# Seam between routing and experts: zeros in TensorE's waits, expert 0's weight blocks loaded in routing, the read of the output's row numbers written behind expert 2

## The chip, the cores and the metric

The program runs on 1 core of one Trainium2 chip. The metric is the time of one execution on the device in microseconds (us); of several runs the median is given. Engines are written as in the profile: PE is TensorE's matmul, PEld its weight load, DVE is VectorE, ACT ScalarE, POOL GpSimd, SP SyncE, whose queue issues most of the DMA. L12 is line 12 of the kernel.

## What is computed

Three stages follow one another; between them nothing leaves the device.

```python
def _attn_ref(q, k, v, s):                 # q, k, v (4, 8, 576, 64), s (4, 8, 576)
    scores = scale * np.matmul(q, k.transpose(0, 1, 3, 2))
    cum = np.cumsum(np.maximum(s, 0.0), axis=-1)
    bias = -(cum[:, :, :, None] - cum[:, :, None, :])
    scores = np.where(causal, -1000000000.0, scores + np.minimum(bias, 0.0))
    attn = softmax(scores)
    return np.matmul(attn, v)

def _moe_ref(x, w_gate, w1, w2):           # x (2304, 512), 8 experts, w1 (8, 512, 1024), w2 (8, 1024, 512)
    cap = N // E                           # 288 tokens for each expert
    for idx in np.argsort(-(x @ w_gate).flatten()):
        tok, e = idx // E, idx % E
        if assigned[tok] < 0 and counts[e] < cap:
            assigned[tok] = e; counts[e] += 1
    for e in range(E):
        out[assigned == e] = np.maximum(x[assigned == e] @ w1[e], 0.0) @ w2[e]

def _moe2_ref(x, w_in, w_out):             # w_in (512, 2048), w_out (2048, 512)
    h = x @ w_in
    return (h * (1.0 / (1.0 + np.exp(-1.702 * h)))) @ w_out
```

`w_in` and `w_out` arrive as 64-bit floats, which the kernel takes apart as pairs of 32-bit integers.

## The kernel before, in words

**Attention and routing.** The first 230 us or so compute attention and write its 2304 rows (each batch padded to 580 rows, five tiles of 116) to `x_rows` in DRAM. Routing then finds, for each expert, the cut above which its 288 tokens lie: rounds of comparisons on VectorE (L468 to L479) and small matmuls on TensorE (L624, L631). `fill_slots` (from L688) turns the assignment into a list: matmuls for positions (L696 to L698), tables `inv` and `lane` on VectorE, ScalarE and POOL (L710 to L717), 20 matmuls that turn them into row numbers (`pid`, L721), and `gather(0)` (L665), three indirect DMAs of POOL that fetch the 288 rows of expert 0. Then it issues matmuls of zeros (`pulse`, L682 to L686: a 128 x 128 block of zeros times 128 x 512 zeros, results not used). While routing computes, SP loads blocks 0 and 1 of expert 0's weights (`load_w`, L498) and two pieces of `w_in` (`first64`).

**Seam.** Behind routing `output_rows` (L760) works out where each row of the result goes, and SP writes these 2304 four-byte numbers to `o_rows` in DRAM (L767). They are read back in another layout into `oids` (L971). The numbers are wanted only at the very end of the kernel, when rows are scattered to the output.

**Experts.** For each expert e the gathered rows are transposed in three groups (`gather_t`, L866) and split into a high and a low half (`xT`: ScalarE L868, VectorE L869). The hidden layer is made in eight column blocks m: `up(e, m)` (L876) issues 12 first products (three products of halves for each of four blocks of the inner dimension; for e = m = 0 smaller ones), ScalarE takes the relu's high half (L891), VectorE the low half `hT` (L892). `down(e, m)` (L895) issues 12 second products (L899) into four PSUM banks. Weights come in four blocks g = m // 2 of 512 KB for w1 and 512 KB for w2; `weights(e, g)` splits them into halves (ScalarE L774, VectorE L775), and their raw tiles `wraw` have four buffers. Beside this run conversions of `w_in` and `w_out` ("jobs"): a DMA of a raw piece (L798, tile `raw64`, two buffers), five integer steps on VectorE (L801 to L810) and one on ScalarE (L804), and a split into halves `win`. Products of `up` and the transposes share four PSUM banks named h, used in turn. So a group of transposes waits until VectorE has read the bank that it is given.

**What sets the order.** Routing up to `fill_slots` is in an order written by hand (`manual_schedule`). From the seam on, the order on each engine, SP's and POOL's queues included, is set by a scheduler that goes by priorities, the text's order and its own cost estimates; the text's place of a DMA is only a hint. Each engine then runs its list in order.

Of the kernel before, what the change touches and what calls it, by code (L numbers as in the profile page):

```python
# [8 lines left out]
F32 = mybir.dt.float32  # L9
# [29 lines left out]
JS = 96  # L39
# [8 lines left out]
def tile_kernel(ctx, tc, qt, kt, v, s, w_gate, w1, w2, w_in, w_out, out):  # L48
# [446 lines left out]
    raws = {}  # L495

    def load_w(e, g):
        r1 = wp.tile([128, 4, 256], F32, name="wraw", bufs=4)  # L498
        if (e, g) == (0, 2):

            G.tensor_copy(r1[:JS, 0, :1], xT["g", 2][:, :1])
        SY.dma_start(r1, w1[e, :, g * 256:(g + 1) * 256].rearrange("(k p) f -> p k f", p=128))
        r2 = wp.tile([128, 2, DM], F32, name="wraw", bufs=4)
        SY.dma_start(r2, w2[e, g * 256:(g + 1) * 256].rearrange("(k p) f -> p k f", p=128))
        raws[e, g] = r1, r2

    load_w(0, 0)
    load_w(0, 1)

    first64 = []  # L510
    for g in range(2):
# [147 lines left out]
    xT = {}  # L659
# [23 lines left out]
    def pulse(n, start=False, W=128):  # L683
        p = rps.tile([128, 512], F32, name="warm", bufs=1) if rps else warm[0]
        for i in range(n):
            PE.matmul(p[:, :4 * W], zeros, zeros[:, None, :W].to_broadcast([128, 4, W]), start=start and i == 0, stop=bool(rps) and i == n - 1)  # L686

    def fill_slots(check=True):  # L688
# [8 lines left out]
        PE.matmul(pos, tri, oh, start=False, stop=False)  # L697
        PE.matmul(pos, ones, incl, start=False, stop=True)  # L698
        if check:
            V.tensor_reduce(cnt, all_, axis=AX.X, op=OP.add)  # L700
        V.tensor_tensor(sl, pos, oh, op=OP.mult)
        if check:
# [158 lines left out]
    def gather_t(e):  # L861
        x = wp.tile([128, 2, 4, CAP], F32R, name="xT")
        for j in range(3):
            p = bank("h")[:, :4 * JS].rearrange("p (d j) -> p d j", d=4)
            for d in range(4):
                PE.transpose(p[:, d], xT["g", 3 * e + j][:, d * 128:(d + 1) * 128], identf[:JS, :JS])  # L866
            o = slice(j * JS, (j + 1) * JS)
            hi = A.activation(x[:, 0, :, o], p, AF.Copy)  # L868
            lo = V.tensor_tensor(x[:, 1, :, o], p, f32(x[:, 0, :, o]), op=OP.subtract)  # L869
        xT[e] = x  # L870
        return hi, lo
# [62 lines left out]
    jobs_ = run_jobs(wp, PM)  # L934
    ws[0, 0] = weights(0, 0)
    warm = [bank("h")]
    pulse(2, True)
    for ins in gather_t(0):
        ctx.enter_context(tc.issue_after(ins.ins))
    for e in range(E):  # L940
        py = [bank(f"y{d}")[:, :CAP] for d in range(4)]
# [25 lines left out]
            A.activation(yt[:, d], py[d], AF.Copy)  # L967
        SY.dma_start(y_dram[:, :, e * CAP:(e + 1) * CAP], yt)
        yt = new_yt()
        if e == 0:  # L970
            SY.dma_start(oids, o_rows.rearrange("(c p) o -> p (c o)", p=128))  # L971
        if e in (0, 1):
            for f in load_y(e, wp):
# [286 lines left out]
```

## Time and profile before

| | |
|---|---|
| runs | 901.83, 906.05, 905.21 us; median 905.21 |
| profiled execution | 903.1 us; span from first to last instruction 901.3 us; mean granted clock of TensorE 0.962 |
| busy, share of the span | PE 94%, DVE 80%, ACT 56%, POOL 31% |
| DMA | 124.37 MB, mean 138 GB/s |
| expert 0's first product to its last group of first products | 272.3 to 309.05 us |

The span is divided into stages with different limits; attention ends near 230 us, routing near 264, the seam near 272, the experts follow one another at some 27 us each, and the second MLP comes last. Busy shares over the whole span say little about the seam; for that one reads timelines (start, duration, engine, line, operation, result and operands, and behind it in brackets how long the engine stood idle before it and what released it) and windows (busy time of each engine in a stretch, the granted TensorE clock as a share of full speed, and the share and rate of DMA).

### The profile page before, as it was taken

To read this page: it belongs to the slowest core of one execution; us is meant where nothing else is said; L and a number is where in the kernel's file an instruction comes from. 1 tells how busy PE (TensorE), PEld (TensorE's weight loads), DVE (VectorE), ACT (ScalarE), POOL (GpSimd) and SP (SyncE) were. 2 spreads that over 40 slices of the span, in tenths; PEclk is the share of its full clock that TensorE was granted. 3 is DMA by queue.
4 is the path that set the end of the run, shared out by engine and by line. 5 is a ranking of instruction groups with operands and counts; after the bars stand their busy time and mean duration, and the time that the engine had idled before them with its cause. 6 is when DMAs were issued, how large, how long until landed. Compare 5 with 4: busy or idle time off the path is not lost.

```text
span 901.3 us, 18540 instructions
## 1 busy us (share of the span) xinstructions
PE 844.4 (94%) x6838; PEld 825.6 (92%) x6838; DVE 723.0 (80%) x1683; ACT 508.7 (56%) x1141; POOL 277.3 (31%) x264
## 2 busy tenths in 40 slices
PE   4899999999559899999999999999999999999997
PEld 3799999999438899999999999999999999999996
DVE  4688888889774679889998589998877987777775
ACT  5899998988433457666575343434435444444432
POOL 2999999973241110031100011111000211111112
PEclk9799999999657799999999999999999999999999
DMA  6886549520517778888875433323255211111101
GB/s 155 195 204 184 147 118 235 126 80 1 166 34 125 231 234 272 254 255 264 259 227 191 138 106 106 111 72 123 83 184 195 84 48 47 48 48 48 48 24 48
DMA packets 88389, 124.37 MB, mean 138 GB/s; under 512 B 10540, under 2 KB 56768, under 8 KB 87780
## 3 DMA queue, kind: packets, MB, share of 16 engines
q1 hardware_dynamic: 85156, 113.55, 43.2%
q0 software_dynamic: 3136, 9.57, 3.5%
q8 instruction: 56, 0.92, 0.4%
q14 instruction: 41, 0.34, 0.1%
HBM read 96.61 MB, written 22.21 MB: 132 GB/s over the span
## 4 chain that ended last, share of the span: by engine, by line
PE 43%; DVE 13%; DMA 5%; issue 5%; ACT 3%; POOL 1%; POOLq 0%; DVEq 0%; SPq 0%; ACTq 0%
PE h L1002 13%; PE y L1034 10%; PE y L899 9%; PE h L889 9%; DVE g L1020 3%; DVE gT L1212 2%; ACT gT L1208 1%; DMA wraw<-in_moe_w_dram 1%; DMA raw<-in_moe_w_in_dram 1%; DMA raw<-in_moe_w_out_dram 1%; DVE g L1014 1%; DMA wi_dram<-wist 1%; DVE part L1065 1%; DVE tmp L1065 1%; PE h L866 1%
## 5 line engine op out<-in xcount | busy, mean ns | idle before, releaser
L1002 PE MATMUL h<-yc,win 128*128 128x256 f32 x1728 | 218.6, 283 | 0.0
L1002 PEld LDWEIGHTS h<-yc,win 128*128 128x128 f32 x1728 | 212.4, 192 | 0.0
L1034 PE MATMUL y<-wout,gT 128*128 128x256 f32 x1491 | 189.6, 282 | 6.8 <-DVE part L1065 4.2
L1034 PEld LDWEIGHTS y<-wout,gT 128*128 128x128 f32 x1491 | 180.8, 189 | 9.4 <-issue 3.5
L1208 ACT ACTIVATE gT<-g 128x896 fp32r<-128x896 f32 x72 | 68.4, 949 | 139.6 <-DVE g L1020 138.7
L889 PE MATMUL h<-xT,w1s 128*128 128x288 f32 (+2 forms) x776 | 119.3, 303 | 4.0 <-DVE w1s L775 3.9
L899 PE MATMUL y<-hT,w2s 128*128 128x288 f32 x768 | 116.3, 300 | 0.9 <-DVE hT L892 0.5
L889 PEld LDWEIGHTS h<-xT,w1s 128*128 128x128 f32 x776 | 111.1, 196 | 4.9 <-DVE w1s L775 4.4
L899 PEld LDWEIGHTS y<-hT,w2s 128*128 128x128 f32 x768 | 107.8, 192 | 1.5 <-DVE hT L892 1.0
L217 DVE TENSOR_TENSOR phl<-pt,phl 116x464 fp32r<-116x464 f32 (+1 forms) x128 | 76.1, 598 | 27.1 <-ACT phl L212 26.9
L1212 DVE TENSOR_TENSOR gT<-g,gT 128x896 fp32r<-128x896 f32 x72 | 78.8, 1095 | 16.4 <-ACT gT L1208 16.3
L1020 DVE TENSOR_TENSOR g<-g 128x128 f32<-128x128 f32 x284 | 75.2, 306 | 4.9
L228 PE MATMUL pt<-phl,vhl 116*128 116x232 f32 (+2 forms) x512 | 76.1, 292 | 1.7 <-POOL vhl L92 1.6
L665 POOL DMA_INDIRECT xg<-x_rows,idx x24 | 29.7, 1237 | 146.7 <-PE h L866 139.5
L212 ACT ACTIVATE phl<-pt 116x464 fp32r<-116x464 f32 (+1 forms) x128 | 69.1, 540 | 9.9 <-PE pt L206 9.7
L228 PEld LDWEIGHTS pt<-phl,vhl 116*128 116x128 f32 x512 | 67.0, 195 | 3.2 <-POOL vhl L92 2.2
L1069 POOL DMA_INDIRECT out_dram<-part,oids x18 | 22.3, 1237 | 150.4 <-DVE part L1065 150.4
L1009 ACT ACTIVATE sg<-h 128x256 f32<-128x256 f32 x84 | 32.0, 383 | 64.0 <-PE h L1002 62.5
L206 PE MATMUL pt<-identf,pr 116*116 116x116 f32 x480 | 65.8, 268 | 0.7 <-DVE phl L217 0.7
L1010 DVE TENSOR_TENSOR g<-h,sg 128x256 f32<-128x256 f32 x84 | 35.5, 423 | 32.8 <-ACT sg L1009 32.3
L165 PE MATMUL sc<-x 128*116 128x348 f32 (+3 forms) x192 | 44.9, 343 | 15.5 <-ACT x L115 11.1
L206 PEld LDWEIGHTS pt<-identf,pr 116*116 116x116 f32 x480 | 51.5, 141 | 4.1 <-PE sc L174 1.0
(192 smaller groups left out, 1427.8 us busy)
## 6 DMA issues: line engine op xcount, KB each, us to landing
wraw<-in_moe_w_dram SPq DMA_DIRECT2D x64, 512.0 KB
yraw<-y_dram SPq DMA_DIRECT2D x18, 512.0 KB
raw<-in_qt_dram SPq DMA_DIRECT2D x30, 290.0 KB
raw<-in_kt_dram SPq DMA_DIRECT2D x30, 290.0 KB
raw<-in_moe_w_in_dram SPq DMA_DIRECT2D x32, 256.0 KB
raw<-in_moe_w_out_dram SPq DMA_DIRECT2D x32, 256.0 KB
y_dram<-yt SPq DMA_DIRECT2D x8, 576.0 KB
vraw<-in_v_dram SPq DMA_DIRECT2D x16, 280.0 KB
```

The source lines that it names most:

```text
L165: PE.matmul(p[:, c0:c0 + w], X[x][:, 0, t * P:(t + 1) * P], X[x][:, 1, k0:k0 + w], start=x == 0 and banks[m] not in banks[:m], stop=x == 1 ...
L206: PE.transpose(p[:, w - P:w], pr[:, place(t, c):place(t, c + 1)], identf[:P, :P])
L212: A.activation(hl[:, 0], p, AF.Copy)
L217: st["lo", i] = V.tensor_tensor(hl[:, 1], st["pt", i, g], f32(hl[:, 0]), op=OP.subtract)
L228: PE.matmul(p[:, t0 * P:(t0 + n) * P], vhl[:, hh, c].rearrange("p a d -> p (a d)"), st["phl", i, g][:, x, col:col + n * P], start=x == 0 a ...
L889: PE.matmul(p[:, o], w[:, a, k, c], x[:, b, k, o], start=n == 0 and (e, m) != (0, 0), stop=n == len(steps) - 1)
L899: PE.matmul(py[d], w[:, a, m % 2, d * 128:(d + 1) * 128], h[:, b], start=m == 0 and n == 0, stop=m == 7 and n == 2)
L1002: PE.matmul(h, w[:, a, k], yc[c][:, b, k], start=n == 0 and (both is None or half == 0), stop=n == 11 and (both is None or half == 1))
L1020: V.tensor_tensor(g[:, o], g[:, a], g[:, b], op=op)
L1034: PE.matmul(acc[b][:, o * 256:o * 256 + 256], t[:, j, x], wout[:, p, i, y], start=p == 0 and n == 0 and b not in banks[:m], stop=end and n ...
L1208: A.activation(t[:, 0, :n], src, AF.Copy)
L1212: V.tensor_tensor(t[:, 1, :n], src, f32(t[:, 0, :n]), op=OP.subtract)
```

## The change

Blocks 2 and 3 of expert 0's weights go into tiles that are free at that time: one of the tag `comb` and one of the tag `xT`. They are so loaded in routing with blocks 0 and 1. A small copy on POOL (L501), which tied the load of block 2 to the gathered rows, is gone. Seven zeros matmuls are put behind the position matmuls of `fill_slots`, one more (three in place of two) ahead of the first transposes, and four, one and two behind the three groups of transposes of expert 0; the zeros and transposes there are held in the text's order on TensorE. The read of `o_rows` is written behind expert 2 in place of expert 0.

```diff
     def load_w(e, g):
-        r1 = wp.tile([128, 4, 256], F32, name="wraw", bufs=4)
-        if (e, g) == (0, 2):
-
-            G.tensor_copy(r1[:JS, 0, :1], xT["g", 2][:, :1])
+
+        spare = {(0, 2): ("comb", 1), (0, 3): ("xT", 2)}.get((e, g))
+        if spare:
+            both = wp.tile([128, 2, 1024], F32, name="wraw_" + spare[0], tag=spare[0], bufs=spare[1])
+            r1, r2 = both[:, 0].rearrange("p (k f) -> p k f", k=4), both[:, 1].rearrange("p (k f) -> p k f", k=2)
+        else:
+            r1 = wp.tile([128, 4, 256], F32, name="wraw", bufs=4)
+            r2 = wp.tile([128, 2, DM], F32, name="wraw", bufs=4)
         SY.dma_start(r1, w1[e, :, g * 256:(g + 1) * 256].rearrange("(k p) f -> p k f", p=128))
-        r2 = wp.tile([128, 2, DM], F32, name="wraw", bufs=4)
         SY.dma_start(r2, w2[e, g * 256:(g + 1) * 256].rearrange("(k p) f -> p k f", p=128))
         raws[e, g] = r1, r2
 
     load_w(0, 0)
     load_w(0, 1)
+    load_w(0, 2)
+    load_w(0, 3)
...
         PE.matmul(pos, ones, incl, start=False, stop=True)
         if check:
+            pulse(7, True)
+        if check:
             V.tensor_reduce(cnt, all_, axis=AX.X, op=OP.add)
...
                 PE.transpose(p[:, d], xT["g", 3 * e + j][:, d * 128:(d + 1) * 128], identf[:JS, :JS])
+            if e == 0:
+                pulse((4, 1, 2)[j])
             o = slice(j * JS, (j + 1) * JS)
...
     warm = [bank("h")]
-    pulse(2, True)
-    for ins in gather_t(0):
+    with tc.manual_schedule(engines={PE.engine}):
+        pulse(3, True)
+        first_split = gather_t(0)
+    for ins in first_split:
         ctx.enter_context(tc.issue_after(ins.ins))
...
-        if e == 0:
+        if e == 2:
             SY.dma_start(oids, o_rows.rearrange("(c p) o -> p (c o)", p=128))
```

SP's queue in the seam, before. (`wraw_4818` and `wraw_4821` are block 2 of expert 0, `wraw_4895` and `wraw_4897` its block 3, `wraw_4983` block 0 of expert 1; `raw64` are pieces of `w_in`.)

```order
L767 DMA o_rows_4707<-oidx_4706 96x24x1
L502 DMA wraw_4818<-in_moe_w1_dram 128x4x256
L504 DMA wraw_4821<-in_moe_w2_dram 128x2x512
L971 DMA oids_4708<-o_rows_4707 128x18x1
L502 DMA wraw_4895<-in_moe_w1_dram 128x4x256
L504 DMA wraw_4897<-in_moe_w2_dram 128x2x512
L502 DMA wraw_4983<-in_moe_w1_dram 128x4x256
L798 DMA raw64_4959<-in_moe2_w_in_dram 128x4x128
L798 DMA raw64_5059<-in_moe2_w_in_dram 128x4x128
```

The same stretch of SP's queue in the changed kernel. (`wraw_5007` and `wraw_5008` are block 0 of expert 1, `wraw_5146` and `wraw_5147` its block 1.)

```order
L774 DMA o_rows_4729<-oidx_4728 96x24x1
L506 DMA wraw_5007<-in_moe_w1_dram 128x4x256
L507 DMA wraw_5008<-in_moe_w2_dram 128x2x512
L982 DMA oids_4730<-o_rows_4729 128x18x1
L506 DMA wraw_5146<-in_moe_w1_dram 128x4x256
L507 DMA wraw_5147<-in_moe_w2_dram 128x2x512
L805 DMA raw64_4983<-in_moe2_w_in_dram 128x4x128
L805 DMA raw64_5083<-in_moe2_w_in_dram 128x4x128
```

Blocks 2 and 3 of expert 0 are gone from it and blocks 0 and 1 of expert 1 stand in their places; one load fewer stands ahead of the third `raw64`. The read of `oids` stands behind the same number of loads as before.

VectorE around the conversion of the third piece of `w_in`, before. (`hT_4918` is the low half for m = 4, `hT_4956` for m = 5; `w1s_4899` is the split of block 3's w1, `w2s_4826` of block 2's w2.)

```order
L801 TENSOR_SCALAR u64_4961<-raw64_4959 128x256
L805 SCALAR_TENSOR_TENSOR u64_4961<-raw64_4959,u64_4961 128x256
L775 TENSOR_TENSOR w1s_4899<-wraw_4895,w1s_4899 128x1024
L807 SCALAR_TENSOR_TENSOR u64_4961<-raw64_4959,u64_4961 128x256
L775 TENSOR_TENSOR win_4729<-w64_4927,win_4729 128x4x64
L775 TENSOR_TENSOR w2s_4826<-wraw_4821,w2s_4826 128x1024
L810 SCALAR_TENSOR_TENSOR w64_4967<-t64_4963,u64_4961 128x256
L892 SCALAR_TENSOR_TENSOR hT_4918<-h_4905,hT_4918 128x288
```

The same in the changed kernel. (`hT_4942` is the low half for m = 4, `hT_4980` for m = 5; `w1s_4923` is block 3's w1, `w2s_4854` block 2's w2, `raw64_4983` the third piece.)

```order
L782 TENSOR_TENSOR w1s_4923<-wraw_xT_3634,w1s_4923 128x1024
L782 TENSOR_TENSOR win_4751<-w64_4907,win_4751 128x4x64
L817 SCALAR_TENSOR_TENSOR w64_4951<-t64_4947,u64_4945 128x256
L782 TENSOR_TENSOR w2s_4854<-wraw_comb_3631,w2s_4854 128x1024
L901 SCALAR_TENSOR_TENSOR hT_4942<-h_4929,hT_4942 128x288
L808 TENSOR_SCALAR u64_4985<-raw64_4983 128x256
L782 TENSOR_TENSOR win_4751<-w64_4951,win_4751 128x4x64
L812 SCALAR_TENSOR_TENSOR u64_4985<-raw64_4983,u64_4985 128x256
L901 SCALAR_TENSOR_TENSOR hT_4980<-h_4967,hT_4980 128x288
```

The first step that reads the third piece has moved from ahead of these two weight splits to behind them and behind the low half for m = 4; it stands directly ahead of a `win` half, a second step on the piece and the low half for m = 5.

## Rows read from the trace of the kernel before

**Rows 1.** Windows: stretch, length, busy us (instructions) per engine, granted clock, DMA share, GB/s.

```profile
272.00:280.00 8.00, 8.00 (x37) 7.77 (x36) 3.51 (x6) 3.40 (x7) 2.78 (x3) 0.50 0.63 31
280.00:281.00 1.00, 1.00 (x8) 1.00 (x8) 1.00 (x4) 0.34 (x1) 0.00 (x0) 0.85 0.90 117
297.00:298.00 1.00, 0.00 (x0) 0.00 (x0) 1.00 (x2) 1.00 (x3) 0.00 (x0) 0.68 0.00 0
307.00:308.00 1.00, 1.00 (x8) 1.00 (x7) 1.00 (x3) 0.00 (x0) 0.00 (x0) 0.70 0.91 237
309.00:520.00 211.00, 210.71 (x1628) 210.24 (x1627) 178.32 (x351) 126.45 (x237) 21.73 (x17) 1.00 0.74 231
```

**Rows 2.** Timeline of PE in experts 0 and 1: start, duration, operation, [idle before].

```profile
298.52 2.77 PE L889 MATMUL h<-xT,w1s 128*128 128x288 f32 x10 [3.38 <-DVE w1s L775]
...
302.73 0.90 PE L866 MATMUL h<-identf,xg 96*128 96x96 f32 x4 [0.16 <-issue]
303.34 5.87 PE L899 MATMUL y<-hT,w2s 128*128 128x288 f32 x28
309.05 1.75 PE L889 MATMUL h<-xT,w1s 128*128 128x288 f32 x12
...
331.79 3.98 PE L899 MATMUL y<-hT,w2s 128*128 128x288 f32 x28
335.61 1.75 PE L889 MATMUL h<-xT,w1s 128*128 128x288 f32 x12
```

**Rows 3.** Timeline of PE in the seam.

```profile
261.30 2.20 PE L721 MATMUL pid<-inv,lane 116*96 116x48 bf16 x20 [3.39 <-POOL inv L714]
263.33 3.52 PE L686 MATMUL warm<-zeros 128*128 128x512 bf16 x8
...
268.82 0.52 PE L866 MATMUL h<-identf,xg 96*128 96x96 f32 x4 [0.78 <-DMA xg<-x_rows,idx]
270.82 1.51 PE L866 MATMUL h<-identf,xg 96*128 96x96 f32 x8 [1.47 <-issue]
```

**Rows 4.** Windows of routing and of the last loads of expert 0.

```profile
233.00:248.00 15.00, 7.26 (x75) 5.39 (x75) 11.73 (x55) 5.58 (x18) 6.41 (x10) 0.50 0.78 250
248.00:264.00 16.00, 7.70 (x71) 5.91 (x72) 13.47 (x49) 6.31 (x15) 6.41 (x8) 0.50 0.02 6
289.00:297.00 8.00, 5.62 (x38) 5.17 (x38) 1.95 (x7) 2.27 (x6) 0.00 (x0) 1.00 0.86 262
```

**Rows 5.** Timeline of POOL in the seam.

```profile
264.84 1.07 POOL L665 DMA_INDIRECT xg<-x_rows,idx  x1 [2.32 <-issue]
...
271.45 0.18 POOL L501 COPY wraw<-xg 96x1 f32<-96x1 f32 x1 [3.08 <-DVE orow L765]
```

**Rows 6.** SP's queue in expert 0: start and duration of the issue.

```profile
283.26 0.37 SPq L971 DMA_DIRECT2D oids<-o_rows  x1
283.73 4.83 SPq L502 DMA_DIRECT2D wraw<-in_moe_w_dram  x1
288.67 0.45 SPq L504 DMA_DIRECT2D wraw<-in_moe_w_dram  x1
```

**Rows 7.** SP's waits, 260 to 312 us: total us, times, longest.

```profile
SPq L971 <- DMA o_rows<-oidx: 9.5, 1, 9.5
```

**Rows 8.** Timeline of DVE in expert 0.

```profile
296.58 0.29 DVE L801 TENSOR_SCALAR u<-raw 128x256 int32<-128x256 int32 x1 [6.01 <-DMA raw<-in_moe_w_in_dram]
296.91 0.42 DVE L805 SCALAR_TENSOR_TENSOR u<-raw,u 128x256 int32<-128x256 int32 x1
...
301.09 0.42 DVE L775 TENSOR_TENSOR win<-w,win 128x256 fp32r<-128x256 f32 x1
301.43 0.42 DVE L805 SCALAR_TENSOR_TENSOR u<-raw,u 128x256 int32<-128x256 int32 x1
...
302.23 0.45 DVE L892 SCALAR_TENSOR_TENSOR hT<-h,hT 128x288 fp32r<-128x288 f32 x1
```

**Rows 9.** Timeline of ACT in expert 0.

```profile
291.69 1.06 ACT L774 ACTIVATE w1s<-wraw 128x1024 fp32r<-128x1024 f32 x1 [2.22 <-DMA wraw<-in_moe_w_dram]
```

## Prediction, made before the changed kernel ran

> **What bounds the kernel now.** I read the windows first, then the timelines of the engine that bounds each stretch. From 309 us on TensorE is never free: 210.71 of the 211 us to 520 are busy, at full granted clock [rows 1]. So whatever arrives earlier at 309 shifts the rest of the program, and the question is only how early expert 0 can be done. Its end is marked by the last first-product group (`up(0,7)`), which starts at 309.05 behind the third group of transposes of expert 1 (at 302.73, called T2 here) and 28 second products [rows 2].
>
> Expert 0 is slow for three reasons, each visible in a row. TensorE waited 3.38 us for the weight half `w1s` of block 3, until 298.52 [rows 2]. The granted clock was 0.50 of full (the lower of the two levels, 1.2 GHz) from 272 to 280, while TensorE was busy all of it, and rose at about 280.3 (0.85 in that microsecond); behind the idle stretch it fell again (0.68 in 297 to 298) and rose at 307.6 (0.70 in 307 to 308) [rows 1]. What would expert 0 take without these? The same 28 second products that took 5.71 us there (303.34 to 309.05) took 3.82 us in expert 1 (331.79 to 335.61), 0.1364 us each [rows 2]. From the first product of expert 0 (272.3, where the last transposes of [rows 3] end) to `up(0,7)` stand 84 first products, 72 second ones and 12 transposes of a third of the columns, together 160 such units: 21.8 us at full clock against 36.8 us taken. The difference of 15.0 us is all that can be won here.
>
> **The change, part by part.**
> *Seven zeros behind the position matmuls.* A zeros matmul costs 3.52/8 = 0.44 us [rows 3], at the lower clock that this stretch has [rows 4], so 3.1 us. TensorE stands idle there for 3.39 us, until `inv` of POOL releases it at 261.30 [rows 3]. Cost 0; if POOL were earlier, at most 3.1 us.
>
> *Four loads in routing instead of in the seam.* They are 4 x 524 kB. The loads that stand there now ran at 250 GB/s until about 248; then DMA moved 6 GB/s until 264 [rows 4]. So the four take 2097 kB / 250 GB/s = 8.4 us, until about 256.5, and the gather of expert 0's rows is issued only at 264.84 [rows 5]. Cost 0; the cover is 8 us wide. The two new homes (the tiles of `comb` and of the second `xT`) are wanted again only later, by expert 1. The removed copy on POOL took 0.18 us and nothing waited for POOL there [rows 5]: 0.
>
> *Eight zeros more in the seam (one before the first transposes, 4, 1 and 2 behind the three groups).* The four fall into a wait of 1.47 us between the first and second group [rows 3]: 0.9 us at full clock, nothing lost; at half clock 1.76 us, 0.3 lost. The three behind cost 0.66 us at full clock, 1.3 at half. The gain they may bring is the first half-clock stretch: 8 us of work done in 4. No row shows the clock in the seam with these zeros in it, so both ends are kept: the clock full from 268 on, or as before.
>
> *The waits on blocks 2 and 3.* Their loads are issued some 30 us or more earlier now, so the 3.38 us wait of TensorE goes. Next late is something else, and the order shows what.
>
> *The row numbers of the output.* The text of the program has them behind expert 2, but in SP's queue their read stands where it stood, behind the two loads that follow the writing. SP will be held there as before: 9.5 us until 283.26 [rows 6, 7]. The next load of w1 was then held for 4.83 us more, and w2's followed at 288.67 for 0.45 us [rows 6]; the four transfers ahead of them are alike in number and size in both kernels, so I take the same. The third piece of `w_in` (`raw64`) now stands behind those two and is issued at 289.2. In front of it are 2 x 524 kB, with its own 262 kB 1311 kB, which at the 262 GB/s of 289 to 297 [rows 4] takes 5.0 us: it lands at about 294.2 (before: 296.5, where VectorE's first reading of it starts at 296.58 [rows 8]).
>
> *Who waits for that piece.* VectorE runs in order. Before, its conversion stood in front of the last weight splits; now it stands in front of the low half of `hT` for m = 5, and T2 needs the PSUM bank that this reads. Behind the landing come the conversion's first step, a `win` half, the second step and `hT`: by the starts of such rows 3 x 0.33 us, and 0.45 us for the last [rows 8], in sum 1.45. So T2 starts at about 295.6, not at 302.73: this **new wait** takes the place of the old one. In before too `hT` for m = 5 ended at 302.68, T2 starting 0.05 us later [rows 2, 8].
>
> *From T2 to `up(0,7)`.* Three cases. (A) The zeros keep the clock up: TensorE has 132 units less, so it is at T2 at 272.3 + 0.66 + 18.0 = 291.0, stands 4.6 us idle, the clock falls as it did behind the idle stretch of 3.38 us, and T2 to `up(0,7)` takes the 6.32 us of before [rows 2]: 301.9, a gain of 7.1. (B) The zeros don't help: TensorE is at T2 at about 295.1, hardly idle, and the 28 products run at full clock: 295.6 + 4.4 = 300.0, a gain of 9.1. (C) As B, and the zeros themselves delay the first product by 1.3 us at half clock: about 301.1, a gain of 8.0. The two half-clock stretches trade against the new wait, so all three lie close: I take 8.0.
>
> *Where the sum stands.* The profiled execution took 903.1 us (span 901.3), 2.1 below the median of 905.21. 903.1 - 8.0 = 895.1, and with the 2.1 us 897.2. From A and B, and 0.7 for the DMA rate, the forecast's own range is 895.5 to 899.5.
>
> The Trainium skill ("Trainium Kernel Development and Optimization", Key Constraints) says that DMAs of all queues run on the same 16 engines and interleave. If the pieces behind it in the queue shared the rate with the third piece of `w_in`, it would end with the fourth, 262 kB later. This case's rows bear that out only in part: w1 of block 3, issued by 288.56, was used at 291.69 [rows 9], 3.1 us on, while 524 kB alone take 2.0 us and all that was issued up to 290.7 needs until 296.5.
>
> **The rivals.**
> 1. *The landing is shared.* The piece lands together with the one behind it, 262 kB or 1.0 us later, at 295.2; T2 and `up(0,7)` follow by 1.0 to 1.2: 898.4. For it: four transfers are in flight at once. Against it: the row on w1 just named.
> 2. *No new wait.* SP was held 4.83 us with w1's buffer long read, so that hold may belong to the queue's state and be shorter now. With the piece issued below 284.5 it lands before TensorE wants T2. With the clock up: 272.3 + 0.66 + 21.8 = 294.8, a gain of 14.2: 891.0. Against it: the same write and the same two loads are in front.
> 3. *Part is lost.* The piece lands at 296.5 as before, T2 starts at 298.0, `up(0,7)` 6.32 us later at 304.3: a gain of 4.7, 900.5. Or the clock falls in the new wait and stays down for some 7 products after `up(0,7)` has begun, 0.14 us each: near 901 as well. For it: in before the clock needed until 307.6, 9 us from the work's start at 298.5.
> 4. *Slower.* One mechanism: SP. Everything that VectorE waits for now hangs behind the reading of the row numbers. Break-even is `up(0,7)` at 309.05, that is T2 at 302.7 and the piece landing at 301.2; from 305.7 on the kernel is over 0.5% slower. If the 9.5 and 4.83 us of holding both last twice as long, because the loads in the seam compete with four-byte writes, the piece lands at 294.2 + 14.3 = 308.5 and the time is 903.1 + 7.3 + 2.1 = 912.5. For it: 9.5 us for a 9 kB write is long already. Against it: the seam now has fewer, not more, bytes that are wanted.
> 5. *The change does less than it says.* For the row numbers that is already so by the order, and counted in the sum. A load that could not start in routing would be seen as a wait at 284; the rows of POOL and DMA give no reason.
>
> **How the numbers follow.** The forecast (A to C) has 0.50, rival 1 0.10, rival 2 0.10, rival 3 0.20, rival 4 0.08, and 0.02 is left for what I don't see. 0.5% is 4.5 us, about what a measurement of this kernel can tell from no change: faster means below 900.7, slower above 909.7. Faster takes the forecast, rivals 1 and 2 and a third of rival 3: 0.76. Same takes the rest of rival 3 and what I don't see, 0.16; slower 0.08. The range runs from rival 2 (891.0, 0.5 below for its clock) to the upper side of rival 3 without the tail: 890.5 to 902.5. It leaves out rival 4, some of rival 3, and little else.
>
> **What would show it right or wrong.** Right: TensorE's 3.38 us wait on `w1s` gone; SP reads the row numbers near 283 and issues the third `raw64` near 289; VectorE waits on that piece until about 294; T2 near 295.6 and `up(0,7)` between 300 and 302, with the second products of the other experts at 0.136 us each. The granted clock of 272 to 280 tells A from B and C. Wrong: T2 before 292 (rival 2), after 297 (rival 3), after 302.7 (rival 4), or a shift at 309 that isn't there at the end, which would mean that a later stage waits for something other than TensorE (VectorE first: it is busy 178 of the 211 us [rows 1]).

## The result, and the profile after

| | before | after |
|---|---|---|
| median | 904.42 us (901.83 to 906.05, 4 runs) | 896.55 us (894.43 to 896.64, 4 runs) |
| ratio on record | | 0.9892, 95% interval 0.9864 to 0.9919 |
| profiled execution | 903.1 us, span 901.3 | 896.56 us, span 894.8 |
| mean granted clock | 0.962 | 0.973 |

By the medians the kernel became faster by 7.9 us (quotient 0.9913); the ratio on record, 0.9892, is not that quotient and would be 9.8 us, so the gain is known to some 2 us. 8.0 us were forecast, from the median of three runs of before (905.21) to 897.2; a fourth run has since brought that median to 904.42. The two profiled executions can't be laid over each other as they stand: attention ended at different times. A mark that the change doesn't touch is SP's last write of `x_rows`, ahead of routing's last rounds. SP's queue before:

```profile
232.08 0.75 SPq L280 DMA_DIRECT2D x_rows<-xs  x2
```

SP's queue after, with the same mark and the seam:

```profile
233.85 0.75 SPq L280 DMA_DIRECT2D x_rows<-xs  x2
...
273.37 0.33 SPq L774 DMA_DIRECT2D o_rows<-oidx  x1
273.80 1.40 SPq L506 DMA_DIRECT2D wraw<-in_moe_w_dram  x1
275.29 0.46 SPq L507 DMA_DIRECT2D wraw<-in_moe_w_dram  x1
283.71 0.37 SPq L982 DMA_DIRECT2D oids<-o_rows  x1
284.18 5.67 SPq L506 DMA_DIRECT2D wraw<-in_moe_w_dram  x1
289.96 0.45 SPq L507 DMA_DIRECT2D wraw<-in_moe_w_dram  x1
290.51 0.96 SPq L805 DMA_DIRECT2D raw<-in_moe_w_in_dram  x2
```

The executions differ by 1.77 us at the mark, so every time of the prediction is to be read 1.8 us later here, and the two spans lie only 6.5 us apart. SP is held for the row numbers until 283.71 and then for 5.67 us more, as in [rows 6], where it was 4.83; the third piece of `w_in` is issued at 290.51 (forecast 289.2 + 1.8 = 291.0). VectorE after, from the reading of that piece on:

```profile
295.57 0.36 DVE L808 TENSOR_SCALAR u<-raw 128x256 int32<-128x256 int32 x1 [6.49 <-DMA raw<-in_moe_w_in_dram]
295.86 0.41 DVE L782 TENSOR_TENSOR win<-w,win 128x256 fp32r<-128x256 f32 x1
296.18 0.41 DVE L812 SCALAR_TENSOR_TENSOR u<-raw,u 128x256 int32<-128x256 int32 x1
296.52 0.44 DVE L901 SCALAR_TENSOR_TENSOR hT<-h,hT 128x288 fp32r<-128x288 f32 x1
```

This is the new wait: 6.49 us of idle VectorE behind the DMA, then the four steps that were counted at 1.45 us, from 295.57 to T2 at 297.02. TensorE after (L873 are transposes, L898 first and L908 second products, L691 zeros):

```profile
271.21 1.91 PE L691 MATMUL h<-zeros 128*128 128x512 bf16 x4
...
274.49 4.79 PE L898 MATMUL h<-xT,w1s 128*128 128x192 f32 x36
...
292.93 0.82 PE L873 MATMUL h<-identf,xg 96*128 96x96 f32 x8
297.02 0.55 PE L873 MATMUL h<-identf,xg 96*128 96x96 f32 x4 [3.26 <-DVE hT L901]
297.35 5.48 PE L908 MATMUL y<-hT,w2s 128*128 128x288 f32 x28
302.66 1.76 PE L898 MATMUL h<-xT,w1s 128*128 128x288 f32 x12
```

The wait of 3.38 us on `w1s` [rows 2] is gone, and one of 3.26 us on `hT` stands in its place. `up(0,7)` starts at 302.66. From the mark to it 68.81 us went by where before had 76.97: 8.16 us won, and from there to the end 592.14 us against 592.25, so nothing is lost or won later. Windows of after (columns: stretch and length, busy us of PE, PEld, DVE, ACT, POOL, clock, DMA share, GB/s):

```profile
248.00:264.00 16.00, 9.36 (x70) 5.95 (x70) 13.20 (x50) 5.85 (x15) 6.06 (x8) 0.51 0.49 156
264.00:270.00 6.00, 3.34 (x23) 1.62 (x23) 1.71 (x6) 0.46 (x1) 3.23 (x4) 1.00 0.19 49
270.00:273.00 3.00, 2.69 (x11) 1.45 (x10) 2.86 (x7) 0.49 (x1) 1.39 (x2) 0.57 0.38 117
274.00:297.00 23.00, 19.75 (x155) 19.42 (x153) 13.35 (x26) 10.29 (x19) 3.68 (x4) 1.00 0.80 151
298.00:301.00 3.00, 3.00 (x14) 3.00 (x13) 3.00 (x6) 1.79 (x6) 1.69 (x1) 0.50 0.58 167
302.00:520.00 218.00, 218.00 (x1693) 218.00 (x1692) 187.72 (x373) 129.89 (x243) 22.65 (x18) 1.00 0.72 226
```

The clock is full (2.4 GHz) from 264 to 270, at the lower level (1.2 GHz) for some 3.5 us while the zeros and transposes of the seam run, and full from the first products of expert 0 on: 36 of them take 4.79 us, before 8.40. It falls once more behind the new wait, for some 3.5 us (before some 10). In 248 to 264 DMA now moves the two blocks, 156 GB/s where it moved 6 [rows 4].

### The profile page after: what moved, and what is told of

It reads as the page before. It is cut to its first block, busy times and chain, and to the rows that moved or that the text cites. A ratio compares the mean times of both kernels' runs of the same rounds, so it can differ in the third digit from the quotient of the medians.

```text
span 894.8 us, 18574 instructions
## 1 busy us (share of the span) xinstructions
PE 840.4 (94%) x6853; PEld 821.0 (92%) x6853; DVE 723.6 (81%) x1683; ACT 509.0 (57%) x1141; POOL 276.8 (31%) x263
## 4 chain that ended last, share of the span: by engine, by line
PE 48%; DVE 12%; issue 4%; ACT 3%; DMA 2%; POOL 1%; SPq 0%; POOLq 0%; DVEq 0%; ACTq 0%
PE h L1013 13%; PE y L1045 11%; PE y L908 11%; PE h L898 11%; DVE g L1031 3%; DVE gT L1223 3%; ACT gT L1219 2%; DVE g L1025 2%; DVE part L1076 1%; PE h L873 1%; DVE tmp L1076 1%; DMA wi_dram<-wist 1%; DVE u L814 1%; DMA raw<-in_moe_w_in_dram 1%; DVE yc L941 1%
## 5 line engine op out<-in xcount | busy, mean ns | idle before, releaser
L908 PE MATMUL y<-hT,w2s 128*128 128x288 f32 x768 | 115.8, 299 | 0.0
L898 PE MATMUL h<-xT,w1s 128*128 128x288 f32 (+2 forms) x776 | 114.2, 295 | 0.0
L908 PEld LDWEIGHTS y<-hT,w2s 128*128 128x128 f32 x768 | 107.4, 191 | 0.0
L898 PEld LDWEIGHTS h<-xT,w1s 128*128 128x128 f32 x776 | 106.5, 188 | 0.1
```

Of the source, the lines that this page charges most:

```text
L898: PE.matmul(p[:, o], w[:, a, k, c], x[:, b, k, o], start=n == 0 and (e, m) != (0, 0), stop=n == len(steps) - 1)
L908: PE.matmul(py[d], w[:, a, m % 2, d * 128:(d + 1) * 128], h[:, b], start=m == 0 and n == 0, stop=m == 7 and n == 2)
```

## The experiments

All runs, each against the kernel before on the same chip; its median there stands in the third column. The ratio is the estimate on record; the quotient of the two medians differs from it by up to 0.2%. "To up(0,7)" counts from the mark in the profiled execution, "rest" from there to the end of the span. These two come from one execution each. The mark itself stood anywhere from 231.92 to 237.75 us in these executions, though nothing ahead of it was changed, and the change, profiled twice, differs by 1.6 us in "to up(0,7)".

| run | median us | before there | ratio (95% interval) | to up(0,7) | rest |
|---|---|---|---|---|---|
| before, profile above | 904.42 | | 1 | 76.97 | 592.25 |
| the change | 896.55 | 904.42 | 0.9892 (0.9864 to 0.9919) | 68.81 | 592.14 |
| the change again, another chip | 900.64 | 907.76 | 0.9942 (0.9912 to 0.9971) | 70.41 | 591.87 |
| loads only | 903.34 | 908.14 | 0.9938 (0.9915 to 0.9960) | 74.89 | 593.78 |
| zeros only | 899.59 | 908.14 | 0.9914 (0.9891 to 0.9936) | 70.94 | 591.81 |
| loads, VectorE's order kept | 897.99 | 907.32 | 0.9910 (0.9875 to 0.9945) | 68.65 | 593.17 |
| row numbers read late | 899.76 | 908.14 | 0.9903 (0.9874 to 0.9933) | 67.57 | 594.06 |
| row numbers written and read late | 904.21 | 908.14 | 0.9946 (0.9925 to 0.9967) | 65.32 | 602.26 |
| both behind the last expert | 892.45 | 907.32 | 0.9838 (0.9808 to 0.9868) | 63.70 | 594.88 |
| written by ScalarE's queue | 899.45 | 907.32 | 0.9895 (0.9853 to 0.9936) | 72.73 | 595.61 |
| before, both behind the last expert | 895.95 | 907.32 | 0.9876 (0.9848 to 0.9904) | 65.78 | 593.39 |
| both behind the last expert, no extra zeros | 898.26 | 907.76 | 0.9888 (0.9860 to 0.9917) | 66.74 | 597.58 |
| zeros, both behind the last expert, no early loads | 892.28 | 907.76 | 0.9832 (0.9803 to 0.9861) | 63.67 | 595.82 |
| both in the second MLP | 893.82 | 907.76 | 0.9845 (0.9817 to 0.9873) | 63.27 | 590.98 |

My theory at the start: the end of expert 0 is set by the third piece of `w_in`, which SP issues late because it is held for the row numbers. Its rival: the early loads, or the clock, carry the gain by themselves.

**Loads only.** The change without its extra zeros.

```diff
-        if check:
-            pulse(7, True)
...
-            if e == 0:
-                pulse((4, 1, 2)[j])
...
-    with tc.manual_schedule(engines={PE.engine}):
-        pulse(3, True)
-        first_split = gather_t(0)
-    for ins in first_split:
+    pulse(2, True)
+    for ins in gather_t(0):
```

> The change without its zeros: blocks 2 and 3 of expert 0 are loaded in routing, the extra zeros (7 in routing, 8 in the seam) are left out. Theory (the time is set by the landing of the third piece of w_in and by what stands behind its first reading on VectorE): in this order VectorE reads that piece ahead of the low half of hT for m = 3 and of the split of block 3, not only ahead of m = 5. It lands near 294 to 296, TensorE then has 56 of its 160 units left, 7.6 us at full clock and 15 at half, so up(0,7) starts at 303 to 310 and the ratio to before is 0.993 to 1.000: most of the gain is lost, though no load is late. Rival (the loads carry the gain, zeros only heat the clock, which the new wait hides): ratio as the whole change, 0.989, give or take 0.002.

Ratio 0.9938, inside the theory's 0.993 to 1.000; the rival's 0.987 to 0.991 lies below the interval. VectorE:

```profile
298.26 0.29 DVE L806 TENSOR_SCALAR u<-raw 128x256 int32<-128x256 int32 x1 [10.25 <-DMA raw<-in_moe_w_in_dram]
298.47 0.45 DVE L897 SCALAR_TENSOR_TENSOR hT<-h,hT 128x288 fp32r<-128x288 f32 x1
```

TensorE, waiting for that `hT` (m = 3):

```profile
298.98 3.01 PE L904 MATMUL y<-hT,w2s 128*128 128x288 f32 x11 [5.90 <-DVE hT L897]
```

No load of expert 0 is late any more, yet in this execution three quarters of the gain up to `up(0,7)` is gone (2.08 us are left of 8.16): without the zeros in the text the scheduler puts the reading of the third piece ahead of `hT` for m = 3. The runs say less: their ratio keeps over half of the gain (0.0062 of 0.0108), and the profiled execution is one of the slower ones. Zeros thus act in two ways, on the clock and on the scheduler's plan.

**Zeros only.** The kernel before with the same zeros lines added.

```diff
+        if check:
+            pulse(7, True)
...
+            if e == 0:
+                pulse((4, 1, 2)[j])
...
-    pulse(2, True)
-    for ins in gather_t(0):
+    with tc.manual_schedule(engines={PE.engine}):
+        pulse(3, True)
+        first_split = gather_t(0)
+    for ins in first_split:
```

> Before with the change's zeros (7 in routing, 8 more in the seam, transposes and zeros in the text's order), loads as before. Theory: block 3's w1 lands near 292 as before, its split no longer stands behind the reading of the third piece of w_in on VectorE, so TensorE goes on near 294 in place of 298.5; the piece lands at 296.5, T2 starts at 298, up(0,7) at 302.4 to 304.3 in place of 309.05: ratio 0.993 to 0.995. Rival (the loads carry the gain): TensorE waits for block 3 until 298.5 as before, ratio 0.999 to 1.001. Third possibility: zeros delay the gathered rows' transposes by 1 to 2 us at half clock, ratio 1.002.

Ratio 0.9914: somewhat better than the theory's 0.993 to 0.995, far from the rival's 0.999 to 1.001. The place of the wait was a miss. TensorE:

```profile
290.15 0.85 PE L893 MATMUL h<-xT,w1s 128*128 128x288 f32 x2 [4.53 <-ACT w1s L776]
```

It waited for block 2, loaded in the seam, and not for block 3; the third piece then came in time. With TensorE at full clock the seam's loads are the bound, and with the loads early the third piece is: each part alone runs into its own wait.

**Loads, VectorE's order kept.** To part the two effects of the zeros: loads only, with two conversions held behind `hT` for m = 4.

```diff
-                f = next(jobs_, None)
-                if f:
-                    f()
+                with tc.issue_after(last_lo[0].ins) if e == 0 and m == 4 else ExitStack():
+                    f = next(jobs_, None)
+                    if f:
+                        f()
```

> The change without its extra zeros (as the run with the loads only), but with the conversion of the second and third piece of w_in held behind the low half of hT for m = 4 on VectorE, as the changed kernel has it for the third. Theory (the zeros' gain over the loads alone came for the most part from the other order on VectorE that they led the scheduler to): TensorE no longer waits 5.9 us for hT of m = 3; T2 comes with the third piece, 63 to 65 us after the last write of x_rows, up(0,7) at 68 to 71 (loads only 74.9, the change 68.8), ratio 0.988 to 0.991. Rival (the zeros' gain was the clock): up(0,7) at 73 to 75, ratio 0.993 to 0.995.

VectorE, at the third piece:

```profile
296.55 0.29 DVE L806 TENSOR_SCALAR u<-raw 128x256 int32<-128x256 int32 x1 [3.68 <-DMA raw<-in_moe_w_in_dram]
296.88 0.43 DVE L810 SCALAR_TENSOR_TENSOR u<-raw,u 128x256 int32<-128x256 int32 x1
297.22 0.45 DVE L897 SCALAR_TENSOR_TENSOR hT<-h,hT 128x288 fp32r<-128x288 f32 x1
```

TensorE, first products and T2:

```profile
274.05 8.58 PE L894 MATMUL h<-xT,w1s 128*128 128x192 f32 x36
...
297.73 0.55 PE L871 MATMUL h<-identf,xg 96*128 96x96 f32 x4 [0.52 <-DVE hT L897]
298.06 3.94 PE L904 MATMUL y<-hT,w2s 128*128 128x288 f32 x28
302.43 1.86 PE L894 MATMUL h<-xT,w1s 128*128 128x288 f32 x12 [0.44 <-DVE hT L897]
```

This is case B of the prediction nearly to the figure: the first products run at half clock (8.58 us), TensorE reaches T2 hardly idle, and the 28 products take 3.94 us. `up(0,7)` comes at 68.65 us, the change has it at 68.81, and the ratios agree (0.9910 and 0.9892, intervals overlapping). So in the change the zeros' clock gained nothing that was kept; it turned into the wait of 3.26 us. (The ratio of the loads only, 0.9938, can't be told from 0.9910 by the runs; what tells the two orders apart is the wait of 5.90 us that is gone.)

**Row numbers read late.** The change, with the read tied on SP behind expert 2's store, so that it does move.

```diff
-        SY.dma_start(y_dram[:, :, e * CAP:(e + 1) * CAP], yt)
+        stored = SY.dma_start(y_dram[:, :, e * CAP:(e + 1) * CAP], yt)
         yt = new_yt()
         if e == 2:
-            SY.dma_start(oids, o_rows.rearrange("(c p) o -> p (c o)", p=128))
+            with tc.issue_after(stored.ins):
+                SY.dma_start(oids, o_rows.rearrange("(c p) o -> p (c o)", p=128))
```

> The whole change, and the read of the output's row numbers tied on SP's queue behind the store of expert 2's result, so that it does leave the seam. Theory: SP is no longer held near 283.7 for the row numbers, the third piece of w_in is issued near 283 to 285 and lands near 289, VectorE doesn't wait for it, T2 follows the two groups before it at once (near 293.8 where the changed kernel had 297.02) and up(0,7) starts near 298 in place of 302.66: 4.5 to 5 us less than the change, ratio to before 0.983 to 0.985. Rival a: the queue is held by the writing of the row numbers, not by their reading, and the piece still lands near 293 or later: ratio 0.987 to 0.989. Rival b: what is won at T2 is lost behind it (VectorE or a weight block becomes the bound in expert 1): ratio 0.988 to 0.990 with T2 near 294.

Rival a in mechanism, though the ratio of 0.9903 lies just above its 0.987 to 0.989. SP's queue of this run:

```profile
282.84 2.40 SPq L507 DMA_DIRECT2D wraw<-in_moe_w_dram  x1
285.40 3.82 SPq L805 DMA_DIRECT2D raw<-in_moe_w_in_dram  x2
```

VectorE at that piece:

```profile
296.89 0.29 DVE L808 TENSOR_SCALAR u<-raw 128x256 int32<-128x256 int32 x1 [5.55 <-DMA raw<-in_moe_w_in_dram]
```

From the mark on the piece was issued 7.6 us earlier than in the change (285.40 less 236.37, against 290.51 less 233.85), but it landed 11.5 us behind its issue in place of 5.1. My theory had the wrong culprit: taking the reading away lets SP issue earlier, but the loads are still slow; that leaves the writing, which the next runs test.

**Row numbers written and read late.** The run before, with the write behind expert 1's store.

```diff
-        ins = SY.dma_start(o_rows.rearrange("(c p) o -> p (c o)", p=JS), oidx)
...
+        if e == 1:
+            with tc.issue_after(stored.ins):
+                SY.dma_start(o_rows.rearrange("(c p) o -> p (c o)", p=JS), oidx)
         if e == 2:
```

> As the run before it, and the writing of the row numbers is moved too, behind the store of expert 1's result: nothing of the row numbers is left in the seam. Theory: the writing costs the seam nothing that TensorE waits for, ratio as that run, within 0.001. Rival: the 2304 four-byte writes hold up the loads behind them (DMA share 0.62 at 51 GB/s from 272 to 280), so this run is 2 to 5 us faster than that run, ratio 0.979 to 0.983.

In the seam the rival was right: `up(0,7)` at 65.32, no wait at T2. But the run lost 10 us later (rest 602.26) that neither theory had. TensorE, in expert 1, some 20 us behind the write:

```profile
357.33 1.54 PE L872 MATMUL h<-identf,xg 96*128 96x96 f32 x8 [7.76 <-DVE hT L900]
```

VectorE there:

```profile
355.34 1.23 DVE L940 TENSOR_TENSOR yc<-yraw,yc 128x1024 fp32r<-128x1024 f32 x1 [10.70 <-ACT yc L939]
```

SP's queue there, the write and the load of `yraw` behind it:

```profile
336.16 0.62 SPq L982 DMA_DIRECT2D o_rows<-oidx  x1
...
342.16 0.57 SPq L936 DMA_DIRECT2D yraw<-y_dram  x1
```

ScalarE waited 11.63 us for that load, until 354.25, and VectorE's order did the rest. Where the write is followed by its reading in the queue, SP waits for it for 7.8 to 9.5 us, in the seam and behind the last expert alike; what matters is who stands behind it. Four windows of 10 us follow, the first three from the write on. The change:

```profile
274.00:284.00 10.00, 10.00 (x80) 9.85 (x79) 7.09 (x12) 5.20 (x9) 1.84 (x2) 1.00 0.81 67
```

The run with the late read:

```profile
276.00:286.00 10.00, 10.00 (x80) 9.78 (x78) 7.01 (x13) 5.38 (x9) 1.84 (x2) 1.00 0.68 57
```

The run with the write on ScalarE's queue (below):

```profile
271.00:281.00 10.00, 5.70 (x23) 3.56 (x21) 3.85 (x5) 4.86 (x7) 3.49 (x3) 0.67 0.74 49
```

The run with both behind the last expert (below), which has no write in the seam:

```profile
274.00:284.00 10.00, 10.00 (x80) 10.00 (x79) 7.28 (x14) 5.27 (x9) 0.95 (x2) 1.00 0.83 246
```

The DMA engines are as busy in the change as without the write (0.81 against 0.83) but move 67 GB/s in place of 246. The Trainium skill ("DMA: Bandwidth & Descriptors", Specifications) says that pieces below 512 bytes don't reach the line rate; the trace agrees: with 2304 pieces of four bytes among the loads the engines were 0.68 to 0.81 busy for 10 us and moved 49 to 67 GB/s.

**Both behind the last expert.** The change, with write and read behind the last store.

```diff
-        if e == 2:
-            SY.dma_start(oids, o_rows.rearrange("(c p) o -> p (c o)", p=128))
+        if e == E - 1:
+            with tc.issue_after(stored.ins):
+                SY.dma_start(o_rows.rearrange("(c p) o -> p (c o)", p=JS), oidx)
+                SY.dma_start(oids, o_rows.rearrange("(c p) o -> p (c o)", p=128))
```

> The whole change, with writing and reading of the output's row numbers both moved behind the store of the last expert's result, where DMA moves 100 GB/s and less. Theory (the 2304 four-byte writes are what holds up the loads behind them, wherever they stand): up(0,7) comes as early as with both moved behind experts 1 and 2 (65.3 us after the last write of x_rows, where the changed kernel has 68.8), and no weight block is late behind it: some 3.5 us better than the change, ratio to before 0.984 to 0.987. Rival: the pieces of w_in and w_out behind the numbers in the queue come late there and TensorE waits for their conversion: ratio 0.990 to 0.995.

The theory held: 0.9838, `up(0,7)` at 63.70, 1.6 us earlier than forecast.

```profile
296.62 1.76 PE L897 MATMUL h<-xT,w1s 128*128 128x288 f32 x12
```

VectorE's order up to the low half for m = 5 is that of the change, so the order is no rival here; VectorE begins on the third piece at 287.97 without having waited for it, 55.05 us from the mark where the change has 61.72. Expert 0 takes 23.16 us from its first product to `up(0,7)`, against 21.8 worked out for full clock. A part of the rival is there too: one wait of TensorE in the second MLP.

```profile
518.83 4.06 PE L1046 MATMUL y<-wout,gT 128*128 128x256 f32 x21 [3.07 <-DVE tmp L1077]
```

**Written by ScalarE's queue.** The change, with the write in the seam through another queue, and the read behind the last store.

```diff
-        ins = SY.dma_start(o_rows.rearrange("(c p) o -> p (c o)", p=JS), oidx)
+        ins = A.dma_start(o_rows.rearrange("(c p) o -> p (c o)", p=JS), oidx)
```

> The whole change, with the row numbers written in the seam as before but through ScalarE's DMA queue in place of SP's, and read behind the last expert's store. Theory a (loads are held because they stand behind the four-byte writes in one queue): the loads of expert 1's blocks 0 and 1 and the third piece of w_in land as early as without the write, up(0,7) 65 to 66 us after the last write of x_rows, ratio 0.984 to 0.987. Theory b (the four-byte writes take the DMA engines themselves, whatever queue they come from): loads late as with the write on SP's queue, up(0,7) at 67 to 69, ratio 0.988 to 0.991.

0.9895, and neither theory as written: the ratio is theory b's, `up(0,7)` at 72.73 is later than both. The write went out at 270.59, ahead of the loads, and TensorE then waited for the gathered rows, which come through POOL's queue:

```profile
278.07 0.87 PE L873 MATMUL h<-identf,xg 96*128 96x96 f32 x4 [4.18 <-DMA xg<-x_rows,idx]
```

So transfers of another queue were late here while the write was under way, the last of them issued at 268.71 (in the change at 269.21, and there TensorE did not wait for it); this speaks for theory b. Behind its first product this execution lost nothing to a late load (26.85 us to `up(0,7)`, most of the excess at half clock). The runs spread from 891.6 to 903.6 us, the profiled one is the slowest of the six, and one profile can't say whether the others were held in the same way; that stays open. The Trainium skill ("Trainium Kernel Development and Optimization", Key Constraints) says that DMAs of all queues share the 16 engines and interleave; this wait of 4.18 us agrees with it.

**Before, both behind the last expert.** No early loads, no extra zeros: only the row numbers move.

```diff
-        ins = SY.dma_start(o_rows.rearrange("(c p) o -> p (c o)", p=JS), oidx)
...
-        if e == 0:
-            SY.dma_start(oids, o_rows.rearrange("(c p) o -> p (c o)", p=128))
+        if e == E - 1:
+            with tc.issue_after(stored.ins):
+                SY.dma_start(o_rows.rearrange("(c p) o -> p (c o)", p=JS), oidx)
+                SY.dma_start(oids, o_rows.rearrange("(c p) o -> p (c o)", p=128))
```

> The kernel before with only the row numbers' writing and reading moved behind the last expert's store: loads and zeros as before. Theory: blocks 2 and 3 and the third piece of w_in were late only because of the row numbers, so TensorE's wait of 3.4 us goes without loading in routing, and only the first half-clock stretch is left: up(0,7) 66 to 68 us after the last write of x_rows (before 77.0), ratio 0.987 to 0.990, as much as the whole change brought. Rival (loads in the seam are late by themselves): TensorE still waits for block 2 or 3, up(0,7) at 71 or later, ratio 0.993 or more.

0.9876, as forecast (`up(0,7)` at 65.78 even a little ahead of it): this one move does about as much as the whole change. TensorE, whose wait on block 3 [rows 2] is gone with the loads left in the seam:

```profile
273.88 7.41 PE L888 MATMUL h<-xT,w1s 128*128 128x192 f32 x36
...
299.71 1.75 PE L888 MATMUL h<-xT,w1s 128*128 128x288 f32 x12
```

VectorE's order changed with it and was not held: the split of block 3's w1 (287.42) now stands ahead of the third piece (289.61). The old order would not have held TensorE either, as far as these rows tell: the piece is there at 289.61, two steps and the split take some 1.9 us more, and TensorE comes to block 3 at 293.37.

**Both behind the last expert, no extra zeros.** The diff of the loads only on top of that of both behind the last expert; its core:

```diff
-            pulse(7, True)
...
-                pulse((4, 1, 2)[j])
```

> The change without its extra zeros, with the row numbers moved behind the last expert's store. Theory (with nothing late, TensorE sets the pace, and the zeros are worth the half-clock stretch less their own time): the first 36 products take 7.4 us in place of 4.8, up(0,7) 65 to 66.5 us after the last write of x_rows (with zeros 63.7), ratio 0.985 to 0.988. Rival (without the zeros VectorE reads the third piece of w_in ahead of hT for m = 3, and that still binds): up(0,7) at 67 or later, ratio 0.989 or more.

**Zeros, both behind the last expert, no early loads.** The kernel of the zeros only, with the row numbers moved as above; against the run of both behind the last expert it undoes the loads:

```diff
-    load_w(0, 2)
-    load_w(0, 3)
```

> The kernel before with the change's zeros and the row numbers moved behind the last expert's store; blocks 2 and 3 of expert 0 are loaded in the seam as before. Theory (the loads in the seam were late only because of the row numbers, so loading them in routing is worth nothing once these are gone): up(0,7) 63.5 to 65 us after the last write of x_rows, ratio 0.982 to 0.986. Rival (with TensorE at full clock from the first product the loads come too late again): TensorE waits for block 2 or 3, up(0,7) at 65.5 to 68, ratio 0.987 to 0.990.

**The change again**, unaltered:

> The changed kernel once more, unaltered, on the chip of the three runs beside it. Both theories: ratio to before 0.987 to 0.992.

TensorE without the zeros:

```profile
273.89 8.03 PE L893 MATMUL h<-xT,w1s 128*128 128x192 f32 x36
...
300.32 1.76 PE L893 MATMUL h<-xT,w1s 128*128 128x288 f32 x12
```

TensorE with the zeros and without the early loads:

```profile
277.80 4.78 PE L892 MATMUL h<-xT,w1s 128*128 128x192 f32 x36
...
300.98 1.75 PE L892 MATMUL h<-xT,w1s 128*128 128x288 f32 x12
```

Without zeros 0.9888 and `up(0,7)` at 66.74, 3.0 us later than with them (63.70): now that nothing is late, the zeros' clock is worth its 3 us. Both figures lie just above the theory's range (0.985 to 0.988, 65 to 66.5); the rival is out, since TensorE waits for no `hT` at all between the first product and `up(0,7)`. Without the early loads 0.9832 and 63.67, as forecast: loading in routing is then worth nothing measurable.

The change again gave 0.9942, higher than its first interval and just above what was expected. Its profile does not explain that: T2 waited 5.24 us in place of 3.26, since VectorE had the third piece later, but this execution, 896.05 us, is the fastest of the seven and as fast as those of the first chip; what made the others slower no trace shows. It shows another thing: the clock was full in it from the seam on until the wait ahead of T2, the first 36 products took 4.78 us, and `up(0,7)` came no earlier. By the medians the gain of the change is 7 to 8 us in two comparisons, by the ratios 5 to 10. The rest behind `up(0,7)` differs by up to 4.2 us among the four runs with the numbers behind the last expert. The rows show a part of it, single waits of TensorE of 3.07 and 3.0 us in the second MLP in two of them and of 2.2 and 1.6 us on `hT` in later experts in the others; I did not follow them further.

**Both in the second MLP.** The change, with write and read behind two loads of y far from any job that is due.

```diff
-        SY.dma_start(raw, y_dram[:, :, c % NCH * CH:(c % NCH + 1) * CH])
+        loaded = SY.dma_start(raw, y_dram[:, :, c % NCH * CH:(c % NCH + 1) * CH])
+        if c in (8, 9):
+            with tc.issue_after(loaded.ins):
+                if c == 8:
+                    SY.dma_start(o_rows.rearrange("(c p) o -> p (c o)", p=JS), oidx)
+                else:
+                    SY.dma_start(oids, o_rows.rearrange("(c p) o -> p (c o)", p=128))
```

> The whole change, with the row numbers written behind the eighth load of y in the second MLP and read behind the ninth, two places where SP's queue is free for some 8 us. Theory (where the numbers stood behind the last expert, TensorE lost 3.1 us at 519 to a conversion that they held up, which this place gives back): the seam as in that run, up(0,7) 63.5 to 65.5 us after the last write of x_rows, and 592 to 593 us from up(0,7) to the end in place of 594.9: ratio 0.980 to 0.984. Rival (the numbers cost 3 us at any place): ratio 0.984 to 0.987, with a wait of TensorE or of the scatter behind 640.

In the profile the theory holds: 63.27 us to `up(0,7)`, and the rest takes 590.98 us, 3.9 less than behind the last expert; the wait of 3.07 us is not there, nor is the one behind 640 that the rival named. The ratio, 0.9845, lies just above the theory's range and inside the rival's, so by time the theory is not shown, and the runs can't tell the two places apart (0.9845 against 0.9838, intervals overlapping, on different chips). All three kernels with zeros and with the numbers behind the experts, 892.28 to 893.82 us, are faster than before. That they are faster than the change is shown on the chip where two of them ran beside it (0.9832 and 0.9845 against 0.9942, intervals apart); against its first ratio of 0.9892 the intervals overlap or are barely apart.

## Why the prediction was right, point by point

- **Zeros behind the position matmuls, cost 0.** Right: seven took 3.19 us, and TensorE still waited 0.41 us for POOL.
- **Loads in routing, cost 0.** Right: rounds of routing kept their 8.42 us (241.11, 249.53 and 257.95 for the same step; before 239.28 and 247.70), and DMA had nothing left to move when the gather was issued. What was not foreseen: SP's own issue was held, 2.41 and 2.60 us.
- **Zeros in the seam.** The four took 1.91 us (estimate 0.9 to 1.76), and the first product came 0.45 us later from the mark. They did bring full clock: case A, though the clock was low for 3.5 us in between. The other runs bear it out: with zeros the first 36 products took 4.78 or 4.79 us in seven profiles, 5.47 in the run with both late and 8.45 behind the wait of 4.18 us; without them 7.41 to 8.58 in five.
- **The new wait.** Right in place, releaser and end: landing near 295.6 (forecast 294.2 + 1.8), 1.45 us to T2. TensorE stood idle for 3.26 us (forecast 4.6), for it came there at 293.76 (forecast 291.0 + 1.8) and the piece landed 0.4 us earlier than forecast.
- **T2 to `up(0,7)`.** Case A had 6.32 us here; it took 5.64, since the clock came back after 3.5 us and not after 10. These 0.68 us and the 0.4 us by which the piece was early turned A's gain of 7.1 into 8.16, near the 8.0 that was taken between the cases. So near a hit is in part luck: the second profile of the change gained 6.56.
- **A and B lie close.** Shown by the run with loads and VectorE's order kept, which has no extra zeros: 68.65 against 68.81 us, one execution each.
- **Row numbers.** Right that their read stays where it was and that everything hangs behind them. Wrong in one step: "Everything that VectorE waits for now hangs behind the reading of the row numbers". With the reading alone moved away `up(0,7)` came 1.2 us earlier than in the change, less than the 1.6 us between its two profiles; with the writing moved away as well 3.5 to 5.5 us.
- **Zeros cost nothing and change only the clock** was an unsaid part of the sum. The order fences showed VectorE's order changed, but I put that down to the loads; the run with the loads only, where the third piece stands ahead of `hT` for m = 3, showed that the zeros had a part in it.

Of the rivals, 1 (898.4) and 3 (900.5) can't be told from the forecast by time alone: the first measurement, 894.43 to 896.64 us, lies below both, but the second chip's ratio leaves room for them. The rows decide against both (the piece landed 5.1 us after its issue, as 1311 kB at 262 GB/s need, and T2 came before 298 + 1.8). Rival 2's time, 891.0, is what the kernels with the row numbers moved away came near to. One price of rival 3 is added up wrongly: its second form, seven products at 0.14 us, takes 1.0 us off case A's gain of 7.1 and gives 899.1, not 901. The forecast's own range, from A and B with 0.7 us either way, adds up to 895.4 to 898.8, not to 899.5, and no row gives the 0.7 us. Neither slip changes the outcome.

## What to carry to other kernels

A transfer of 9 kB is not small if it is 2304 pieces of four bytes: look for it in the windows as a high DMA share at a low rate, and put it where nothing that is due stands behind it. That this holds for other queues too is shown by one execution only. When two waits lie close behind each other, removing one or speeding up what is ahead of them buys only the distance to the next; find what both hang on first. Instructions added as filler also change a scheduler's plan on other engines, so an experiment that takes them away has to hold that order fixed.

## What I had not expected of the hardware

The write took some 10 us from its issue to the read behind it (273.37 to 283.71) with the engines 0.81 busy at 67 GB/s, and in one execution transfers of another queue were late beside it as well (4.18 us for gathered rows). The granted clock fell in the change at about 270.4, within the zeros and transposes of the seam, though it had been full since 263.6; TensorE had stood idle for 2.44 us until 269.43. It was full again from 273.8 on. In the second profile of the change the idle stretch there was 1.39 us, and the clock stayed full. After the wait of 3.26 us it came back in 3.5 us, after 5.24 us (second profile) in 3.4, where before it took some 10 behind a wait of 3.38, though TensorE was busy from 298.52 on but for 0.16 us; no run here shows why.
